# A gated-state attention followed by a SoLU layer on one core: v through a third queue, DMA transposes in the last units, a halved last unit and a new order

## The chip, the cores and the metric

One core of a Trainium2 chip runs the whole program. The metric is the device time of one execution in microseconds (us). The core has five instruction streams: TensorE (PE in the profile, with its weight loads as PEld), VectorE (DVE), ScalarE (ACT), GpSimd (POOL) and SyncE (SP). DMA transfers are issued from the queues of SP, ACT and POOL.

## The reference

```
state = 0                                        # per batch b and head h: 48 x 48
for t in range(768):
    cur   = outer(u * k[t], v[t])
    y[t]  = r[t] @ (state + cur)
    state = w[t][:, None] * state + outer(k[t], v[t])
x  = y, heads side by side                       # 3072 tokens x 384
h  = x @ w_in                                    # 384 -> 1024
s  = h * softmax(h)
ln = (s - mean(s)) / sqrt(var(s) + 1e-6) * g_ln
out = ln @ w_out                                 # 1024 -> 384
```

There are 4 batches, 8 heads, 768 steps and a head size of 48. Everything is given and returned in float32.

## The kernel before

The 768 steps are cut into 6 chunks of 128, which with 4 batches makes 24 units; unit i is batch i mod 4 of chunk i div 4. A unit is 128 tokens of all 8 heads, 384 columns. The recurrence of a chunk becomes matrix products.

- The front of a unit. `LW`, `LK`, `LR`, `LV` load its w, k, r and v (192 KB each, in runs of 192 bytes). `lw` takes the logarithm of w, `cum` sums it over time by two triangular matmuls, `ex` takes the exponential in PSUM, `kp` multiplies it into k and r. `krk` and `krr` transpose the results by head pair on TensorE (four matmuls each), and `kr` copies them out of PSUM. `M` forms the 128 x 128 scores of each head; `m` evicts them, with the mask on DVE, or without it on ACT, and then `sel` masks them on POOL. `p`, `q`, `dg` and `dv` build the bonus of u; `vb` rounds v to bf16. `S`, `et` and `st` advance the state. `Y` multiplies scores and state with v, and `y` evicts it and adds dv (or `Y` adds dv by a matmul with the identity, marked i).
- The back of a unit. `X` transposes y on TensorE and `xT` copies it. `H` is the matmul with w_in into 1024 hidden rows; `e` is their exponential, `he` is h times e, and `hq` its square. `Oa` and `Ob` are the two halves of the last matmul, whose one-column matmuls also sum he, e and hq for the mean, the softmax's sum and the variance. `sq`, `qm` and `lv` turn the sums into a scale, `o` applies it at eviction, and `out` stores 128 rows.
- Once. `LI` and `LO` load w_in and w_out, `wi` rounds w_in, `gw` multiplies w_out by g_ln into w2, `mn` forms the mean over its rows by matmuls, `mc` copies that to SBUF, and `ce` subtracts it from w2 in eight pieces. Every `Oa` needs all of w2. `us` and `uc` spread u over partitions. `hot` issues matmuls on zeros that nothing reads.

The order is written out by hand in the string `ORDER` (L21 to L70) and played by the loop at L522: each word is a stage, its unit, and after the dot the engine or queue (s, a, d, p) or the PSUM slot. The class `InOrder` (L75) chains every instruction behind the one before it on its engine, so nothing on one engine overtakes, DMA issues on that engine's queue included.

Buffers are rings: 7 deep for loaded inputs (`NIO`), 10 for lw and vb, 6 for kp, dv and kr, 4 for the rest (L72). A load of unit i+7 waits until unit i's readers are done. PSUM has single-bank slots s0 to s3 and the two-bank slots b0 and b1. The stages `turned_kr` and `turned_x` (L444 and L447) are defined, but the order before doesn't name them.

Of the kernel before, what the change touches and what calls it, by code (L numbers as in the profile page):

```python
# [8 lines left out]
F32 = mybir.dt.float32  # L9
BF16 = mybir.dt.bfloat16  # L10
# [11 lines left out]
LW0.a LK0.s LU0.a LR0.s LW1.a LW2.s hot4.s3 LG0.s LK1.s lw0 LV0.a cum0.b0 LR1.s us0.s0 ex0 hot2.s3 uc0 lw1 LV1.s  # L22
p0 kp0 LW3.a LK2.a LR2.s krk0.s3 q0 krr0 cum1.b1 kr0.a hot2.s2 LV2.s LK3.a M0.b0 LR3.s p1 gs0.s1 ex1 m0.d
hot3.s3 LI1.s lw2 q1 dg0 cum2.b0 lw3 hot2.s3 kp1 vb0.p LI0.a S0.s2 dv0 vb1.a dg1 hot1.s3 ex2 Y0.is0 et0 LV3.a
cum3.b1 LI2.s p2 kp2 krk1.s3 gc0 LO0.s ex3 st0 LW4.s krk2.s1 q2 krr1 LO1.s krr2 kp3 kr1.a hot3.s2 dv1 LK4.s
kr2.d y0.a p3 M1.b0 LK5.a S1.s2 dg2 krk3.s3 vb2.a m1.d krr3 et1 wi0.a S2.s0 wi1.p M2.b1 st1 X0.s1 kr3.a m2.d
Y1.is2 LR4.s wi2.p et2 y1.a M3.b0 xT0.d LV4.a X1.s3 q3 m3.d H0.b1 dv2 gw1.a dg3 gw2.d e0 Y2.is2 LW5.s xT1.d
gw3.p st2 H1.b0 y2.a he0 lw4 gw0.a X2.s1 LR5.s e1 gw7.d cum4.b1 gw4.d hot2.s3 gw6.d gw5.d ex4 he1 vb3.p mn0.s3
LW6.s LV5.a dv3 xT2.a LK6.s kp4 S3.s0 mc0 Y3.is2 LR6.s lw5 ce6.d krk4.s1 ce3.d hq0.a cum5.b0 ce4.d krr4 ce2.d
H2.b1 ce7.d ex5 LW7.s ce1.d ce5.d ce0.d y3.a LK7.s p4 kp5 et3 Oa0.s3 lw6 e2 LR7.s kr4.d p5 krk5.s2 cum6.b0 st3  # L30
hq1.a Ob0 vb4.p he2 LW8.s q4 krr5 ex6 S4.s1 LK8.s kr5.d sq0 M4.b1 lw7 Oa1.s0 kp6 et4 m4.a LR8.s X3.s2 qm0 st4
vb5.p M5.b0 xT3.a cum7.b1 dg4 sel4 lv0 krk6.s1 LV6.s Ob1 m5.d ex7 LW9.s dv4 lw8 S5.s2 kp7 o0.a krr6 LK9.s p6
cum8.b0 sq1 et5 Y4.ns3 kr6.d ex8 H3.b1 q5 LV7.s y4.d hq2.a kp8 q6 LR9.s krk7.s1 e3 X4.s3 st5 LW10.s vb6.p M6.b0
krr7 xT4.d Oa2.s2 dg5 m6.a LK10.s qm1 kr7.d dv5 krk8.s3 lv1 Ob2 he3 out0 sel6 o1.a lw9 M7.b0 out1 dg6 S6.s1 sq2
m7.a LV8.s hq3.d krr8 cum9.b1 LR10.s Y5.ns0 vb7.p qm2 kr8.d lv2 H4.b0 p7 LW11.s et6 y5.d ex9 st6 p8 lw10 kp9
LV9.s X5.s3 S7.s0 e4 Oa3.s1 q7 o2.d vb8.a he4 out2 cum10.b1 dv6 xT5.a krk9.s2 et7 LK11.s ex10 Y6.ns3 q8 krr9 st7
LV10.s H5.b0 hq4.a kp10 sel7 LR11.s kr9.a y6.d M8.b1 dg7 LW12.s S8.s0 lw11 m8.d Ob3 dv7 et8 e5 LV11.s vb9.p
krk10.s3 st8 X6.s2 LK12.s p9 M9.b1 he5 xT6.a Y7.ns0 sq3 m9.a krr10 LR12.s S9.s2 dg8 cum11.b0 et9 LW13.s y7.d
H6.b1 lw12 dv8 ex11 kr10.d LK13.s p10 qm3 lv3 kp11 Oa4.s0 LR13.s e6 q9 st9 X7.s3 cum12.b0 LW14.s xT7.a Ob4 he6
p11 ex12 LV12.s krk11.s2 sel9 sq4 Y8.ns3 o3.a kp12 H7.b1 hq5.a out3 vb10.p qm4 y8.d q10 LK14.s lv4 dg9 M10.b0 e7  # L40
Oa5.s1 LR14.s m10.d vb11.p q11 o4.a krr11 LW15.s X8.s3 lw13 dg10 Ob5 p12 xT8.a out4 he7 kr11.a S10.s0 dv9 S11.s3
LV13.s dg11 sq5 hq6.a Y9.ns2 vb12.p qm5 cum13.b0 y9.d dv10 LK15.s H8.b1 et10 ex13 st10 LR15.s et11 lw14 kp13
Oa6.s2 LW16.s e8 hq7.d krk12.s0 lw15 M11.b0 p13 st11 LK16.s Ob6 lv5 he8 o5.a q12 krr12 m11.a Y10.ns3 out5 kr12.d
krk13.s1 cum14.b1 LR16.s y10.d sq6 krr13 sel11 ex14 cum15.b0 LW17.s kr13.d Oa7.s0 ex15 qm6 LV14.s kp14 p14
Y11.ns3 lw16 X9.s1 Ob7 kp15 lv6 dv11 LK17.s vb13.a xT9.d p15 o6.a M12.b1 y11.d M13.b0 m12.a X10.s1 out6 m13.d
# [12 lines left out]
e15 X16.s2 o12.d Y17.ns0 xT16.a M18.b0 hq14.a y17.d out12 krk20.s3 Ob13 he15 lw22 X17.s0 m18.a krk21.s2 xT17.d
krr20 cum22.b1 dg19 krr21 sq13 sel18 ex22 qm13 S18.s0 dg20 H16.b0 kr20.d hq15.a q21 kr21.d lv13 kp22 Oa14.s3
dv19 e16 dv20 M19.b1 et18 Y18.ns2 he16 m19.a Ob14 lw23 sel19 y18.d M20.b1 sq14 M21.b0 o13.d Oa15.s2 m21.a st18  # L60
out13 m20.d krk22.s1 X18.s0 cum23.b0 xT18.a krr22 Ob15 ex23 hq16.d vb22.p dg21 kr22.a Y19.ns0 q22 kp23 H17.b1
vb23.a dv21 qm14 sq15 y19.d lv14 Y20.ns1 e17 p23 o14.d H18.b0 dg22 out14 sel21 qm15 y20.d lv15 krk23.s0 he17 e18
Oa16.s3 dv22 krr23 o15.a he18 q23 Ob16 kr23.a out15 X19.s1 M22.b1 xT19.d M23.b0 hq17.d X20.s2 S19.s0 xT20.a
hq18.d Oa17.s1 m22.a dg23 Y21.ns2 et19 m23.a sel22 st19 H19.b1 sq16 sel23 qm16 y21.d lv16 Oa18.s0 e19 dv23
X21.s2 Ob17 he19 H20.b0 sq17 o16.d xT21.d out16 Y22.ns3 qm17 e20 Y23.ns2 y22.d Ob18 y23.d hq19.a he20 H21.b1
lv17 o17.d X22.s3 Oa19.s2 e21 out17 xT22.d hq20.d X23.s1 sq18 H22.b0 he21 xT23.d Ob19 qm18 hq21.d e22 H23.b1
sq19 lv18 qm19 he22 Oa20.s3 e23 o18.d hq22.d Oa21.s1 out18 lv19 he23 Ob20 o19.d Ob21 sq20 hq23.d out19 Oa22.s0
sq21 qm20 qm21 lv20 Oa23.s2 lv21 o20.d o21.d out20 Ob22 out21 Ob23 sq22 qm22 lv22 sq23 qm23 o22.d lv23 out22
o23.a out23
# [27 lines left out]
def kernel(  # L97
# [14 lines left out]
    C = 128  # L112
# [20 lines left out]
    def bank(shape, dtype, slot, name):  # L133
# [6 lines left out]
    v_t = ring("v_in", NIO, [C, H, 64], F32)  # L140
# [8 lines left out]
    dve.memset(warm, 0.0)  # L149
    uti_neg = consts.tile([C, C], BF16)  # L150
    pool.memset(uti_neg, -1.0)
    pool.affine_select(out=uti_neg, in_=uti_neg, compare_op=ALU.is_ge, fill=0.0, base=0,
                       pattern=[[1, C]], channel_multiplier=-1)
    uts = consts.tile([C, C], BF16)
    pool.memset(uts, 1.0)
    pool.affine_select(out=uts, in_=uts, compare_op=ALU.is_gt, fill=0.0, base=0,
                       pattern=[[1, C]], channel_multiplier=-1)
    ident_f = consts.tile([C, C], F32)
    pool.memset(ident_f, 0.0)
    pool.affine_select(out=ident_f, in_=ident_f, compare_op=ALU.not_equal, fill=1.0, base=0,  # L160
                       pattern=[[-1, C]], channel_multiplier=1)
# [394 lines left out]
```

The softmax here doesn't subtract the row's maximum and nothing guards it: scores larger than these inputs give would overflow.

## Time and profile before

| what | value |
|---|---|
| three runs | 152.56, 152.88, 152.94 us; median 152.88 |
| profiled execution | 153.27 us, its span 151.6 us |
| busy PE, DVE, ACT, POOL | 137.2, 127.9, 117.9, 94.9 us |
| first output matmul (w2 ready) | 33.73 us |
| SP issues of v, stores | 20 and 24 |
| bytes moved by DMA | 27.08 MB, 179 GB/s mean |

The span runs from the first to the last recorded instruction; the profiled execution's own time is a little longer. A group line gives busy time and the mean of one instruction, then the idle time of the engine ahead of it with what ended it. The chain of work is followed back from the last instruction, at each step to what released it.

### The profile page before, as it was taken

Reading aid. Unit: us, or ns where it says so; the run is one execution under the profiler, and the core shown is the slowest. Engines: PE = TensorE matmul, PEld = TensorE weight load, DVE = VectorE, ACT = ScalarE, POOL = GpSimd, SP = SyncE. Lnnn points to the kernel's source line nnn. Section 1 sums busy time; section 2 is a strip of 40 time slices with the busy share of each in tenths; the row PEclk is TensorE's granted clock in tenths of the full one; section 3 lists DMA queues with packets and bytes.
Section 4 is the critical chain, followed back from the end, with each engine's and each line's share of the span. In section 5 each row is a group of like instructions: output and inputs, shape, how many; then the busy total and the mean of one; then the engine's idle time right before and its main releaser. Section 6 shows DMA issues by size and latency. Waiting matters only on the chain.

```text
span 151.6 us, 5258 instructions
## 1 busy us (share of the span) xinstructions
PE 137.2 (91%) x2156; PEld 106.6 (70%) x2158; DVE 127.9 (84%) x235; ACT 117.9 (78%) x238; POOL 94.9 (63%) x127
## 2 busy tenths in 40 slices
PE   4799787879999997999988999999999999999980
PEld 1145566467788776888777797878887888889650
DVE  5209797999999996999976999999998998688940
ACT  3465766599999997999798688999898997484442
POOL 7484993531879859993849999299847682500000
PEclk9999999999999999999999999999999999999997
DMA  5999999999983999989699999898950111011142
GB/s 110 259 257 334 405 335 255 178 210 188 224 179 121 229 217 193 215 176 241 142 243 208 230 175 232 162 230 193 248 164 6 52 56 52 4 52 56 52 160 104
DMA packets 104825, 27.08 MB, mean 179 GB/s; under 512 B 100313, under 2 KB 104418, under 8 KB 104802
## 3 DMA queue, kind: packets, MB, share of 16 engines
q1 hardware_dynamic: 94256, 24.26, 69.6%
q10 hardware_dynamic: 10546, 2.49, 7.3%
q8 instruction: 17, 0.28, 0.7%
q14 instruction: 6, 0.05, 0.1%
HBM read 22.03 MB, written 4.72 MB: 176 GB/s over the span
## 4 chain that ended last, share of the span: by engine, by line
PE 54%; DMA 12%; SPq 10%; DVE 8%; ACT 6%; POOL 4%; issue 4%; ACTq 0%; POOLq 0%
PE o_ps L89 22%; PE h_ps L89 13%; SPq L89 10%; DMA w_in<-in_w_dram 6%; PE kr_ps L89 4%; PE y_ps L89 4%; DMA kr_in<-in_r_dram 4%; PE s_ps L89 3%; PE cum_ps L89 3%; PE m_ps L89 3%; DMA v_in<-in_v_dram 3%; PE x_ps L89 2%; DVE he L89 1%; POOL m L89 1%; DVE w L89 1%
## 5 line engine op out<-in xcount | busy, mean ns | idle before, releaser
L89 PE MATMUL o_ps<-w,he 128*128 128x385 bf16 x192 | 45.7, 325 | 0.1
L89 PE MATMUL h_ps<-xT,win_sb 128*128 128x128 bf16 x576 | 35.9, 219 | 0.3 <-DVE xT L89 0.3
L89 PEld LDWEIGHTS <-win_sb 128*128 128x128 bf16 x576 | 33.0, 98 | 0.9 <-issue 0.4
L89 PE MATMUL o_ps<-inv_col,e 128*128 128x1 bf16 x192 | 31.7, 165 | 0.0
L89 DVE TENSOR_TENSOR he<-h_ps,e 128x1024 bf16<-128x1024 f32 x24 | 29.1, 1216 | 2.7 <-ACT e L89 2.5
L89 PE MATMUL o_ps<-one_col,hq 128*128 128x1 bf16 x192 | 31.3, 163 | 0.0
L89 ACT ACTIVATE e<-h_ps 128x1024 bf16<-128x1024 f32 x24 | 24.5, 1020 | 4.7 <-PE h_ps L89 4.6
L89 DVE TENSOR_TENSOR kp<-cum_ps,kr_in 128x768 bf16<-128x768 f32 x24 | 22.7, 948 | 5.9 <-ACT cum_ps L89 5.6
L89 PEld LDWEIGHTS <-hq 128*128 128x128 bf16 x192 | 18.5, 96 | 12.8
L89 POOL TENSOR_TENSOR p<-kr_in 128x384 bf16<-128x384 f32 x24 | 24.4, 1018 | 3.7 <-DMA kr_in<-in_r_dram 3.6
L89 POOL TENSOR_TENSOR dv<-vb,dg 128x384 bf16<-128x384 bf16 x24 | 19.8, 830 | 9.6 <-DVE dg L89 7.4
L89 POOL TENSOR_SCALAR_AFFINE_SELECT m<-m 128x1024 bf16<-128x1024 bf16 x15 | 16.8, 1120 | 13.4 <-ACT sq L89 5.8
L89 POOL TENSOR_TENSOR q<-p,u_bc 128x384 bf16<-128x384 bf16 x24 | 21.8, 911 | 1.9 <-ACT u_bc L89 1.7
L89 PEld LDWEIGHTS <-kp 128*128 128x128 bf16 x272 | 17.4, 98 | 6.0 <-DVE kp L89 2.1
L89 ACT ACTIVATE cum_ps<-cum_ps 128x768 f32<-128x768 f32 x24 | 19.2, 802 | 3.0 <-PE cum_ps L89 2.9
L89 PE MATMUL kr_ps<-ident,kp 128*128 128x128 bf16 x192 | 18.0, 222 | 2.3 <-ACT gr L89 0.8
L89 PEld LDWEIGHTS <-he 128*128 128x128 bf16 x192 | 18.4, 96 | 0.9
L89 PEld LDWEIGHTS <-e 128*128 128x128 bf16 x192 | 18.4, 96 | 0.5 <-issue 0.2
L89 ACT ACTIVATE lw<-w_in 128x384 bf16<-128x384 f32 x24 | 12.4, 523 | 4.1 <-DMA w_in<-in_w_dram 4.1
L89 ACT CAST m<-m_ps 128x1024 bf16<-128x1024 f32 x15 | 15.0, 1013 | 0.7 <-PE m_ps L89 0.6
L89 DVE TENSOR_TENSOR m<-m_ps,keep 128x1024 bf16<-128x1024 f32 x9 | 10.9, 1215 | 4.2 <-PE m_ps L89 4.2
L89 ACT ACTIVATE hq<-he 128x1024 bf16<-128x1024 bf16 x13 | 13.7, 1057 | 0.0
(82 smaller groups left out, 262.5 us busy)
## 6 DMA issues: line engine op xcount, KB each, us to landing
kr_in<-in_r_dram SPq DMA_DIRECT2D x24, 192.0 KB, 4.3
out_dram<-o SPq DMA_DIRECT2D x24, 192.0 KB, 3.2
kr_in<-in_k_dram SPq DMA_DIRECT2D x21, 192.0 KB, 3.5
w_in<-in_w_dram SPq DMA_DIRECT2D x21, 192.0 KB, 4.2
v_in<-in_v_dram SPq DMA_DIRECT2D x20, 192.0 KB, 4.1
wout_f<-in_moe_w_out_dram SPq DMA_DIRECT2D x2, 768.0 KB, 7.7
win_f<-in_moe_w_in_dram SPq DMA_DIRECT2D x2, 512.0 KB, 5.1
v_in<-in_v_dram ACTq DMA_DIRECT2D x4, 192.0 KB, 4.2
```

The lines of the kernel that those rows point to most:

```text
L89: made = make(*args, **kwargs)
```

## The change

- v is loaded 11 times from POOL's queue, 8 times from SP's and 5 times from ACT's, into a tile without padding; it stays float32 and is rounded by `vb` as before. 14 of the stores, two pieces of w_in and one of w_out are issued from POOL as well.
- `centre` reads the column mean from PSUM; its copy to SBUF is gone.
- In units 20 to 23, `KD` and `XD` transpose kp and y by DMA from SP's queue, in place of the matmuls `krk`, `krr`, `X` and the copies `kr`, `xT`.
- Unit 23's back is done in halves: `Ha`, `Hb`, with e, he and hq each in two parts; the sums (`Sa`, `Sb`) go to a PSUM slot of their own ahead of the output matmuls, which are split by columns too (`Mal`, `Mar`, `Mbl`, `Mbr`); ACT and DVE evict one half each, and two stores write them.
- u is rounded to bf16 before it is spread. The constants are set by DVE and only cut to shape by POOL; `keep` is `uts`.
- The order is new throughout. Ahead of the first `Oa` it has `H` up to unit 3 and `cum` up to unit 6 (before: 2 and 5). Dummies: 17 in five groups instead of 19 in eight.

```diff
--- before.py
+++ after.py
...
-LW0.a LK0.s LU0.a LR0.s LW1.a LW2.s hot4.s3 LG0.s LK1.s lw0 LV0.a cum0.b0 LR1.s us0.s0 ex0 hot2.s3 uc0 lw1 LV1.s
-p0 kp0 LW3.a LK2.a LR2.s krk0.s3 q0 krr0 cum1.b1 kr0.a hot2.s2 LV2.s LK3.a M0.b0 LR3.s p1 gs0.s1 ex1 m0.d
-hot3.s3 LI1.s lw2 q1 dg0 cum2.b0 lw3 hot2.s3 kp1 vb0.p LI0.a S0.s2 dv0 vb1.a dg1 hot1.s3 ex2 Y0.is0 et0 LV3.a
-cum3.b1 LI2.s p2 kp2 krk1.s3 gc0 LO0.s ex3 st0 LW4.s krk2.s1 q2 krr1 LO1.s krr2 kp3 kr1.a hot3.s2 dv1 LK4.s
-kr2.d y0.a p3 M1.b0 LK5.a S1.s2 dg2 krk3.s3 vb2.a m1.d krr3 et1 wi0.a S2.s0 wi1.p M2.b1 st1 X0.s1 kr3.a m2.d
-Y1.is2 LR4.s wi2.p et2 y1.a M3.b0 xT0.d LV4.a X1.s3 q3 m3.d H0.b1 dv2 gw1.a dg3 gw2.d e0 Y2.is2 LW5.s xT1.d
-gw3.p st2 H1.b0 y2.a he0 lw4 gw0.a X2.s1 LR5.s e1 gw7.d cum4.b1 gw4.d hot2.s3 gw6.d gw5.d ex4 he1 vb3.p mn0.s3
-LW6.s LV5.a dv3 xT2.a LK6.s kp4 S3.s0 mc0 Y3.is2 LR6.s lw5 ce6.d krk4.s1 ce3.d hq0.a cum5.b0 ce4.d krr4 ce2.d
-H2.b1 ce7.d ex5 LW7.s ce1.d ce5.d ce0.d y3.a LK7.s p4 kp5 et3 Oa0.s3 lw6 e2 LR7.s kr4.d p5 krk5.s2 cum6.b0 st3
-hq1.a Ob0 vb4.p he2 LW8.s q4 krr5 ex6 S4.s1 LK8.s kr5.d sq0 M4.b1 lw7 Oa1.s0 kp6 et4 m4.a LR8.s X3.s2 qm0 st4
-vb5.p M5.b0 xT3.a cum7.b1 dg4 sel4 lv0 krk6.s1 LV6.s Ob1 m5.d ex7 LW9.s dv4 lw8 S5.s2 kp7 o0.a krr6 LK9.s p6
...
-X21.s2 Ob17 he19 H20.b0 sq17 o16.d xT21.d out16 Y22.ns3 qm17 e20 Y23.ns2 y22.d Ob18 y23.d hq19.a he20 H21.b1
-lv17 o17.d X22.s3 Oa19.s2 e21 out17 xT22.d hq20.d X23.s1 sq18 H22.b0 he21 xT23.d Ob19 qm18 hq21.d e22 H23.b1
-sq19 lv18 qm19 he22 Oa20.s3 e23 o18.d hq22.d Oa21.s1 out18 lv19 he23 Ob20 o19.d Ob21 sq20 hq23.d out19 Oa22.s0
-sq21 qm20 qm21 lv20 Oa23.s2 lv21 o20.d o21.d out20 Ob22 out21 Ob23 sq22 qm22 lv22 sq23 qm23 o22.d lv23 out22
+LV0.p pc0 LW0.a LK0.s LW1.a LW2.s hot6.s3 LR0.a LW3.s LU0.a LK1.s lw0 cum0.b0 hot2.s3 LW4.s ex0 lw1 LR1.a
+cum1.b1 hot3.s3 ex1 kp0 p0 LK2.s lw2 ur0 LR2.s krk0.s0 us0.s1 LK3.s cum2.b0 uc0 LV1.a krr0 q0 hot3.s3 LR3.s lw3
+kp1 LV2.a LI0.p ex2 LK4.s p1 dg0 krk1.s2 cum3.b1 vb0.a kr0.d hot3.s3 LR4.s lw4 LI1.p kp2 ex3 dv0 LI2.s LG0.a
+M0.b0 S0.s3 q1 m0.d vb1.a krr1 LW5.s krk2.s1 kr1.a p2 krr2 kp3 et0 LV3.a M1.b0 q2 dg1 kr2.a cum4.b1 krk3.s0 m1.d
+p3 Y0.ns2 krr3 ex4 S1.s1 LO0.s y0.d vb2.p kr3.a LK5.s q3 dg2 S2.s2 st0 wi0.a dv1 kp4 X0.s3 M2.b0 et1 LO1.p xT0.a
+dg3 krk4.s0 wi1.a st1 p4 m2.d Y1.is1 wi2.a LR5.s M3.b1 q4 krr4 gs0.s3 m3.d LW6.s gc0 H0.b0 et2 dv2 vb3.a kr4.d
+y1.a LV4.p lw5 Y2.is3 st2 e0 M4.b1 dg4 dv3 S3.s1 LK6.s y2.a he0 gw3.p Y3.is0 m4.a X1.s2 X2.s3 LR6.s et3 xT1.d
+gw0.a gw1.p cum5.b1 xT2.d H1.b0 st3 y3.a ex5 gw2.d LV5.p gw6.d gw5.a gw4.d gw7.d e1 LW7.s kp5 mn0.s2 he1 LK7.s
+lw6 hq0.a krk5.s3 vb4.p cum6.b1 LV6.p X3.s1 ce1 LR7.s krr5 ex6 H2.b0 ce7 sel4 ce3 kr5.a LW8.s kp6 S4.s0 xT3.a
+dv4 ce0 vb5.a krk6.s3 LK8.s H3.b1 et4 ce5 p5 e2 ce6 LR8.s ce2 p6 LV7.a krr6 ce4 Y4.is1 lw7 he2 e3 q5 LW9.s
+Oa0.s2 vb6.p hq1.a LK9.s he3 M5.b0 q6 Ob0 y4.a LR9.s LV8.p m5.a kr6.d cum7.b1 Oa1.s1 hq2.d ex7 LW10.s sel5 st4
+X4.s3 sq0 M6.b0 lw8 kp7 LK10.s Ob1 xT4.a p7 m6.a qm0 dg5 krk7.s0 LR10.s cum8.b1 hq3.d lv0 krr7 S5.s3 sq1 q7 dg6
...
+Y8.ns1 LW16.s e6 p12 Oa5.s0 y8.d st8 kr12.a LK16.s X7.s1 p13 M11.b0 xT7.d S9.s3 dg11 lw14 LR16.s vb10.p Ob5 he6
+m11.a dv9 S10.s2 et9 LW17.s LV12.p hq6.d cum14.b1 et10 sq5 H7.b0 ex14 qm5 st9 LK17.s q12 st10 lv5 kp14 krk13.s1
...
+lv10 he13 Ob11 dv17 ex20 p20 Y15.ns0 o10.a dg18 H14.b0 hq12.a kp20 q20 lw21 y15.d KD20 krk19.s1 LV20.p sq11 e14
+krr18 qm11 Y16.ns0 kr18.d M17.b1 out10.p krr19 y16.d LK23.s m17.a S15.s2 hq13.d LV21.s Oa12.s0 lv11 kr19.d p21
...
+ex21 out11.p H15.b1 qm12 xT16.a p22 kp21 et16 lv12 S17.s2 e15 hq14.d KD21 Y17.ns1 H16.b0 st16 sel18 vb20.a he15
...
+KD22 lw23 he17 hq16.a Y18.ns3 q23 cum23.b0 Y19.ns2 y18.d ex23 M20.b1 dv20 y19.d Oa16.s3 sq14 m20.a kp23 vb21.p
+X18.s2 vb22.p Ob15 qm14 xT18.d KD23 lv14 dv21 X19.s2 sq15 M21.b0 hq17.d H18.b1 m21.a LV23.s xT19.d sel20 o14.d
...
+Ob17 y20.d qm16 m23.d XD20 lv16 Y21.ns1 sel22 H19.b0 o16.a dg23 sq17 et18 vb23.p y21.d dv23 S19.s3 st18 e19 XD21
+Oa18.s1 et19 he19 Y22.ns2 Ob18 y22.d H20.b1 sq18 qm17 qm18 XD22 st19 lv17 hq19.d Y23.ns2 e20 H21.b0 out16 y23.d
+lv18 XD23 he20 Oa19.s3 e21 hq20.d H22.b1 he21 Ob19 e22 o17.d Ha23.b0 out17 sq19 he22 Oa20.s2 ea23 o18.a qm19
+Hb23 hq22.d hq21.a out18 Ob20 Oa21.s0 sq20 lv19 qm20 hea23 o19.a Oa22.s1 eb23 out19.p Ob21 lv20 heb23 hqa23.a
+Ob22 hqb23.d sq21 qm21 o20.d lv21 Sa23.s3 sq22 out20.p qm22 o21.d Sb23 lv22 Mal23.s2 sq23 o22.a out21.p Mar23.s0
+qm23 Mbl23 lv23 out22 Mbr23 ol23.a or23.d outl23.a outr23
 """
...
-    v_t = ring("v_in", NIO, [C, H, 64], F32)
+    v_t = ring("v_in", NIO, [C, H, D], F32)
...
+    ident_f = consts.tile([KF, KF], F32)
...
+    ones_row = consts.tile([1, C], BF16)
...
+    keep = uts
+
+    def constants(i, x):
+        dve.memset(warm, 0.0)
+        dve.memset(uti_neg, -1.0)
+        dve.memset(uts, 1.0)
+        dve.memset(ident, 0.0)
+        dve.memset(ident_f, 0.0)
+        pool.affine_select(out=uti_neg, in_=uti_neg, compare_op=ALU.is_ge, fill=0.0, base=0,
+                           pattern=[[1, C]], channel_multiplier=-1)
+        pool.affine_select(out=uts, in_=uts, compare_op=ALU.is_gt, fill=0.0, base=0,
+                           pattern=[[1, C]], channel_multiplier=-1)
+        pool.affine_select(out=ident, in_=ident, compare_op=ALU.not_equal, fill=1.0, base=0,
+                           pattern=[[-1, C]], channel_multiplier=1)
+        pool.affine_select(out=ident_f, in_=ident_f, compare_op=ALU.not_equal, fill=1.0, base=0,
+                           pattern=[[-1, KF]], channel_multiplier=1)
+        dve.memset(one_col, 1.0)
+        dve.memset(inv_col, 1.0 / RDF)
+        dve.memset(ones_row, 1.0)
+
+        dve.memset(halves, 0.0)
+        dve.memset(off_blocks, 0.0)
+        for row, own in ((0, 0), (32, 1)):
+            dve.memset(halves[row:row + 1, 64 * own:64 * own + 64], 1.0)
+            dve.memset(off_blocks[row:row + 1, :, 1 - own], -30000.0)
+        for j in range(max(NLW, NKP)):
+            if j < NLW:
+                dve.memset(lw_t[j][:, :, D:], 0.0)
+            if j < NKP:
+                dve.memset(kp_t[j][:, :, :, D:], 0.0)
+        dve.memset(mean_w, -1.0 / DF)
+        dve.memset(w2[:, :, DM:], 1.0 / RDF)
...
-    mean_sb = consts.tile([128, DM], BF16)
...
-    queue = {"s": sp, "a": act}
+    queue = {"s": sp, "a": act, "p": pool}
...
-        queue[x].dma_start(out=v_t[i % NIO][:, :, :D], in_=rows_of(v, i))
+        queue[x].dma_start(out=v_t[i % NIO], in_=rows_of(v, i))
...
+    def round_u(i, x):
+        dve.tensor_copy(out=u_b, in_=u_row)
+
-        pe.matmul(ps["u"], lhsT=ones_row, rhs=u_row, start=True, stop=True)
+        pe.matmul(ps["u"], lhsT=ones_row, rhs=u_b, start=True, stop=True)
...
-    def copy_mean(i, x):
-        act.copy(out=mean_sb, in_=ps["mean"])
-
     def centre(f, x):
-        (dve if x == "d" else pool).tensor_add(out=w2[:, f, :DM], in0=w2[:, f, :DM], in1=mean_sb)
+        dve.tensor_add(out=w2[:, f, :DM], in0=w2[:, f, :DM], in1=ps["mean"])
...
+    def hidden_a(i, x):
+        live[i]["h_ps"] = bank([128, KF, C], F32, x, "h_ps")
+        hidden_part(i, 0, KF // 2)
+
+    def hidden_b(i, x):
+        hidden_part(i, KF // 2, KF)
...
+    def columns_of(i, x, side, part):
+        if part == 0:
+            live[i]["o" + side] = bank([C, DM // 2], F32, x, "o_ps")
+        for f in range(part * KF // 2, (part + 1) * KF // 2):
+            pe.matmul(live[i]["o" + side], lhsT=he_t[i % NWK][:, f, :], rhs=w2[:, f, HALF[side]],
+                      start=(f == 0), stop=(f == KF - 1))
+
+    def sums_of(i, x, part):
+        if part == 0:
+            live[i]["sums"] = bank([C, 3], F32, x, "o_ps")
+        to = live[i]["sums"]
+        for f in range(part * KF // 2, (part + 1) * KF // 2):
+            pe.matmul(to[:, 0:1], lhsT=he_t[i % NWK][:, f, :], rhs=w2[:, f, DM:], start=(f == 0), stop=False,
+                      skip_group_check=True)
+            pe.matmul(to[:, 1:2], lhsT=e_t[i % NWK][:, f, :], rhs=inv_col, start=False, stop=False,
+                      skip_group_check=True)
+            pe.matmul(to[:, 2:3], lhsT=hq_t[i % NWK][:, f, :], rhs=one_col[:, :1], start=False, stop=(f == KF - 1),
+                      skip_group_check=True)
...
+        cols = HALF.get(side, slice(0, DM))
+        queue[x or "s"].dma_start(out=out[b * S + c * C:b * S + (c + 1) * C, cols], in_=o_t[i % NWK][:, cols])
...
```

## The prediction

> **What bounds the kernel now.** I read the page first, then busy time in 4 us stretches, then the chain of work that ended last, then the waits. All instructions are recorded at the helper's line 89, so I go by tiles.
>
> ```profile
> span 151.6 us, 5258 instructions
> PE 137.2 (91%) x2156; PEld 106.6 (70%) x2158; DVE 127.9 (84%) x235; ACT 117.9 (78%) x238; POOL 94.9 (63%) x127
> ```
>
> The stretches, with columns length, then busy us of PE, PEld, DVE, ACT and POOL, granted clock, DMA share and GB/s:
>
> ```profile
> 28.00:32.00 4.00, 2.89 (x33) 1.84 (x32) 3.65 (x8) 2.13 (x5) 2.32 (x3) 1.00 0.98 192
> ...
> 80.00:84.00 4.00, 3.30 (x59) 2.75 (x57) 2.85 (x6) 2.81 (x5) 4.00 (x6) 1.00 0.93 209
> ...
> 104.00:108.00 4.00, 4.00 (x66) 3.40 (x65) 3.96 (x8) 3.67 (x9) 4.00 (x5) 1.00 1.00 219
> ...
> 112.00:116.00 4.00, 4.00 (x77) 3.41 (x75) 3.61 (x7) 3.85 (x9) 3.56 (x4) 1.00 0.09 27
> ```
>
> TensorE is full from 32 to 147 us except for about 2.6 us. DVE is nearly full beside it, and the loads end at 112. Before 32, TensorE has room (2.89 of 4) and the DMA engines don't (0.98). So there are two regimes: supply and weight preparation to 33.7 us, then the length of TensorE's queue. The chain of work shows the border, the price of each stage, and the end (columns: start, us, what):
>
> ```profile
> 30.67 0.49 ACT mean_sb L89
> 31.27 0.45 issue
> 31.72 1.97 DVE w L89 x7
> 33.73 0.99 PE o_ps L89 x12
> ...
> 54.22 0.83 PE o_ps L89 x12
> 55.05 0.24 PE kr_ps L89 x4
> 55.30 0.17 PE x_ps L89 x3
> 55.47 0.33 PE m_ps L89 x8
> ...
> 56.50 0.46 PE s_ps L89 x10
> 56.96 0.33 PE cum_ps L89 x2
> 57.28 1.35 PE h_ps L89 x24
> ...
> 62.03 0.37 PE y_ps L89 x12
> ...
> 140.38 5.98 PE o_ps L89 x84
> 146.38 0.18 ACT sq L89
> ...
> 148.20 0.58 ACT o L89
> ```
>
> The first output matmul (Oa0) starts at 33.73, when w2 is centred. The last unit's sums are read at 147.24 by the timeline, so TensorE ends near 147.1; 4.5 us follow (sums, scale and eviction to 148.78, then the store). From the waits (total us, times, longest):
>
> ```profile
> POOL vb L89 <- DMA v_in<-in_v_dram: 6.1, 4, 2.8
> DVE w L89 <- ACT mean_sb L89: 0.4, 1, 0.4
> ```
>
> v arrives late four times, so supply isn't free even at 80 us, where POOL is full and TensorE is not.
>
> **What the Trainium skill says.** "DMA: Bandwidth & Descriptors", Issuing engines are not separate DMA queues: all queues share 16 engines, and more issuers save only issue time. The trace agrees in part: with SP alone the issues take 0.64 to 1.1 us each back to back at about 200 GB/s, while with two queues the first 12 us hold 257 to 259. "SBUF — State Buffer", Who interferes with whom: descriptors for a GpSimd DMA are written by GpSimd itself and stall while DVE holds the shared port. No run of before issues one.
>
> **The change part by part.** I count TensorE stages at the chain's prices: H 1.34, an output half 0.83, krk or krr 0.225, cum 0.33, S 0.46, M 0.33, Y 0.37, X 0.18.
>
> *Order around Oa0.* Walking the old list from Oa0 to the end gives 107.6 us; the trace took 147.1 - 33.7 = 113.4. The excess of 5.8 (2.6 idle, the rest pipeline bubbles) I keep. The new list puts more before Oa0: one H 1.34, cum 0.33, M 0.33, S 0.46, Y 0.37, X 0.18 and two krk with two krr 0.90, together 3.9 us out of the full regime.
>
> *DMA transposes in units 20 to 23* (KD and XD in the list). Four times krk, krr and X leave TensorE: 4 x (0.45 + 0.18) = 2.5 us, and with them 4 copies of kr and 4 of xT leave ACT and DVE. One more Y adds dv by a matmul, +0.16. The transposes go down SP's queue when loads are over. Neither kind is in the trace. "VectorE: DVE Perf Modes", The three transpose paths, prices one 128x128 block at 1.309 us by DMA. KD has 8 blocks, 1.3 us side by side to 10.5 one after the other; TensorE's work between issue and use is 15.9, 11.5, 7.6 and 4.7 us. XD has 3, 1.3 to 3.9; its cover is 4.2, 3.7, 2.5 and 3.0, less the eviction of y (0.55). The loss is 0 to about 2.5 for XD and 0 to 5.8 for the last KD. A store takes 3.2 us to land, so fixed latency counts: I take 1.0 in all.
>
> *Last unit in halves.* Twelve one-column matmuls at 0.025 each half, 0.5 to 0.6 in all, and 16 half-width ones at 0.083 (half of 0.16 and a little), about 1.4, replace 1.66: +0.24. In return sums, variance and scale (147.24 to 148.2) run beside the main matmuls, and ACT and DVE evict half each. After TensorE's end stand 0.35 for half an eviction (0.58 now) and 2.85 for the store as now (148.78 to 151.6): 3.2 instead of 4.5.
>
> So the list after Oa0 is 107.6 - 3.9 - 2.5 + 0.16 + 0.24 = 101.6, with 5.8 excess 107.4. DVE falls by the same count from 102 to 94, ACT from 95 to 89: neither takes over. Kept at zero: the round of u (DVE idles 3.44 before the first kp, and the matmul falls from fp32's 1.64 to about 0.33) and the constants moved to DVE, in the same idle time. Without that cover they cost some 1.5 us.
>
> *When Oa0 starts.* The second half of w_out now stands behind 21 unit loads instead of 16: 5 x 0.197 MB at 260 to 330 GB/s is 3.0 to 3.8 us. A third queue and an idle SP give part back; I take 2.3, so w_out is ready near 26.5 instead of 24.3 (issued at 16.6 at the latest, 7.7 to landing). DVE's work from there: three gains 1.44, two kp 1.75, one he 1.13, and eight centrings from PSUM. Their nearest row is y<-y_ps,dv, 0.548, start to start 0.47, against 0.30 now: 3.8 us. Sum 8.1, no mean_sb copy and issue (0.94 gone), 0.4 for gaps: Oa0 at 35.0. Bounds are 33 (supply no later, transfers faster) and 39 (all the moved work must wait for unit 6's data).
>
> *v and stores from GpSimd's queue.* SP loses 12 v loads, 15 stores and three weight pieces and gains two other loads, a half store and the transposes; v_in is dense on chip. Supply to vb gets earlier, worth 0 to 2 us (the idle at 76 to 84 is 1.4); I put it against new jitter. The cost lies on POOL: 7 transfers before Oa0 are weights, LV0 and LV4 to LV6, and 18 stand between Oa0 and the last dv. The old emission row doesn't exist. "DMA: Bandwidth & Descriptors", Specifications, gives about 1 us to the first byte for this path and calls it emission; a v load has 1024 runs of 192 B, so I bound it by 0.4 and 3 us and take 1.0. POOL's own work in that stretch is 67.4 (74.2 before); TensorE's is 84.8, with its share of excess 89. The slack is 21.7 us, 1.2 per transfer. At 1.0 POOL is 96% full, and behind a late transfer queue p, q, dv, the masks and vb, for which y, Y and S wait. I charge 1.1 us.
>
> Sum: 35.0 + 107.4 = 142.4 for TensorE's end, + 3.2 = 145.6, + 1.0 transposes + 1.1 POOL = 147.7 for the span. The profiled execution took 153.27 with a span of 151.6, and the median is 152.88, 1.28 above the span: 149.0.
>
> **Rivals.** *GpSimd becomes the bound (slower).* Place: between Oa0 and the last dv. Each us per transfer above 1.2 adds 18 us; without my 1.1 the time is 147.9 + 18e - 21.7, and passes 152.9 at e = 1.48. For it: 1024 short runs per v load, DVE full in 104:108, and stores that wait in POOL's queue for an eviction. Against it: 11 of the 18 are stores with 128 runs. With v loads at 2.6 and stores at 1.1, e is 1.7 and the time about 157.
>
> *The start gives it back.* The front work before Oa0 needs unit 6, and in 28:32 the DMA share is 0.98 at 192 GB/s. If Oa0 slips to 38.5, the time is 152.5, no change. For it: w_out later in every queue. Against it: a third queue.
>
> *Transposes block by block.* Then the cover of the last KD and of XD22 and XD23 fails, 8.3 us in all, and the time is 156. Against it: 7.6 us of cover and more for three of four.
>
> *The changes do more than charged*, supply early and Oa0 at 33: 146.
>
> **How the numbers follow.** Forecast 0.50 (146.8 to 151), start 0.13, GpSimd 0.28, transposes 0.06, more 0.03. Within 0.3%, 152.42 to 153.34, is what a measurement can't tell from none: 0.06, mostly from the start's case. Faster is 0.50 + 0.03 + 0.07 = 0.60, slower 0.28 + 0.06 = 0.34. The range runs from 146 to 157.5: about 0.05 lies below and 0.14 above; the forecast's own range is 146.8 to 151.
>
> **What would show it.** Right: o_ps begins near 35 us, kr_ps and x_ps have 160 and 60 matmuls, PE is full to about 143, and sq of the last unit comes before its last o_ps matmul. Wrong: POOL at 9 in every slice from 35 to 125 us, with PE waiting for dv, m or vb; kr_s or xT released by DMA after 120 us; PE idle before o_ps after 36. A PE gap in the start long enough to halve the clock, now that no dummy stands after unit 3's cum, would also break the sum: matmuls of 384 columns would then take 0.5 us, as they do before 13 us, instead of 0.33.

## The result: slower by 9.5%, and the profile after

The changed kernel takes 167.34 us (median of four runs, 167.09 to 168.38), the kernel before on the same chip 152.91: a ratio of 1.095 (95% interval 1.089 to 1.101). I had predicted 149.0, with 146 to 157.5 as the range. The prediction was wrong by 18 us. Some executions of a kernel take over 1.5% longer than its fastest: the ratios leave these out, the medians don't.

The head of the page of the changed kernel: the span, and the busy time of each engine with its share of the span and its instructions.

```profile
span 165.4 us, 5234 instructions
...
PE 138.8 (84%) x2128; PEld 108.5 (66%) x2128; DVE 139.3 (84%) x238; ACT 119.3 (72%) x245; POOL 113.5 (69%) x139
```

The span grew by 13.8 us. TensorE's busy time grew by 1.6 only, and matmuls that ran at half clock for a while are part of that. DVE gained 11.4 and POOL 18.6. POOL at 69% isn't full, so it isn't simply the new bound. The span falls into three pieces:

| piece | before | predicted | after |
|---|---|---|---|
| first output matmul (Oa0) starts | 33.7 | 35.0 | 46.65 |
| from there to TensorE's end | 113.4 | 107.4 | 115.3 |
| after TensorE's end | 4.5 | 3.2 | 3.5 |
| charged for transposes and POOL | | 2.1 | |
| span | 151.6 | 147.7 | 165.4 |

So 12.9 us were lost before Oa0, 1.9 after it, and 1.0 won at the end. Busy time in 4 us stretches shows the places (columns as in the view of before: length, busy us of PE, PEld, DVE, ACT and POOL, granted clock, DMA share, GB/s):

```profile
24.00:28.00 4.00, 3.05 (x32) 2.13 (x32) 3.13 (x5) 3.47 (x8) 3.44 (x4) 0.50 1.12 300
...
36.00:40.00 4.00, 1.03 (x5) 0.35 (x5) 4.00 (x5) 1.00 (x2) 4.00 (x5) 1.00 0.77 153
...
72.00:76.00 4.00, 0.00 (x0) 0.00 (x0) 4.00 (x1) 0.94 (x2) 3.98 (x6) 0.81 0.90 181
76.00:80.00 4.00, 3.21 (x39) 2.12 (x39) 3.18 (x7) 0.00 (x0) 3.98 (x5) 0.50 1.01 214
```

From 24 to 28 TensorE is busy but at half clock. From 36 to 40 it does next to nothing while DVE and POOL are both full. From 72 to 76 it does nothing at all, and DVE's 4.00 us belong to one instruction; then the clock is at 0.50 again. The chain of work that ended last (here in part) names these instructions (start, us, what):

```profile
13.02 7.65 DMA win_f<-in_moe_w_in_dram
...
20.69 0.38 ACTq L88
...
27.54 2.69 PE h_ps L88 x24
...
31.30 1.23 DVE he L88
...
33.52 5.50 DVE w L88 x4
...
69.15 6.91 issue
76.06 0.69 DVE kr L88
```

The first two lines: ScalarE issues the load LV3 only once a piece of w_in has landed, and its own work stands behind that issue. The third: unit 0's `H` takes 2.69 us where before a `H` took 1.34, the half clock. The fifth: four gains on DVE take 5.50 us; before, the first output matmul began where this line begins. "69.15 6.91 issue" is a time in which DVE waited for nothing that the profile shows. DVE's and POOL's own instructions there, from the timeline of the changed kernel (start, us, engine, operation, tiles):

```profile
68.95 7.18 DVE L88 TENSOR_TENSOR hq<-he 128x1024 bf16<-128x1024 bf16 x1
```

```profile
68.47 0.95 POOL L88 DMA_DIRECT2D v_in<-in_v_dram  x1
69.44 1.11 POOL L88 TENSOR_SCALAR_AFFINE_SELECT m<-m 128x1024 bf16<-128x1024 bf16 x1
70.50 1.95 POOL L88 TENSOR_TENSOR p<-kr_in 128x384 bf16<-128x384 f32 x2
72.40 0.49 POOL L88 CAST vb<-v_in 128x384 bf16<-128x384 f32 x1
...
75.47 1.61 POOL L88 TENSOR_SCALAR_AFFINE_SELECT m<-m 128x1024 bf16<-128x1024 bf16 x1
```

This is unit 5's square (`hq`). All squares on DVE, from the tile's view (shortest/median/longest in ns), first before and then in the changed kernel:

```profile
L89 DVE TENSOR_TENSOR hq<-he x11: 674/681/1419, 46.5 to 143.3; 128x1024 bf16<-128x1024 bf16 x11
```

```profile
L88 DVE TENSOR_TENSOR hq<-he x16: 425/692/7184, 48.9 to 158.9; 128x1024 bf16<-128x1024 bf16 x15, 128x512 bf16<-128x512 bf16 x1
```

The longest took 1.42 us before and takes 7.18 now, beside a median of 0.68 and 0.69. POOL runs nine instructions without a gap over it, and the square ends 0.66 us into the mask at 75.47, which itself takes 1.61 instead of 1.1. This is read as DVE's instruction being held until POOL gave way once. The waits of the changed kernel (total us, times, longest) show who stood behind it, and what came before POOL's close row of work:

```profile
POOL m L88 <- ACT m L88: 9.9, 2, 8.3
...
PE y_ps L88 <- DVE kr L88: 6.2, 1, 6.2
```

TensorE waited 6.2 us for the copy of kr that is next in DVE's order. POOL had waited 8.3 us for a mask's input, while Oa0 was late, and from 49.4 us on worked off what had piled up, nearly without a gap.

### The profile page after: what moved, and what is told of

It reads as the page before. It is cut to its first block, busy times and chain, and to the rows that moved or that the text cites. A ratio compares the mean times of both kernels' runs of the same rounds, so it can differ in the third digit from the quotient of the medians.

```text
span 165.4 us, 5234 instructions
## 1 busy us (share of the span) xinstructions
PE 138.8 (84%) x2128; PEld 108.5 (66%) x2128; DVE 139.3 (84%) x238; ACT 119.3 (72%) x245; POOL 113.5 (69%) x139
## 4 chain that ended last, share of the span: by engine, by line
PE 53%; DVE 18%; issue 8%; SPq 7%; DMA 6%; ACT 5%; ACTq 0%; DVEq 0%
PE o_ps L88 18%; PE h_ps L88 17%; SPq L88 7%; DMA win_f<-in_moe_w_in_dram 5%; PE y_ps L88 4%; PE s_ps L88 3%; DVE w L88 3%; PE m_ps L88 3%; PE kr_ps L88 3%; DVE kp L88 3%; DVE he L88 3%; PE cum_ps L88 2%; DVE st L88 2%; DVE hq L88 2%; DMA kr_in<-in_r_dram 2%
## 5 line engine op out<-in xcount | busy, mean ns | idle before, releaser
L88 PE MATMUL o_ps<-w,he 128*128 128x385 bf16 (+2 forms) x208 | 47.3, 317 | 0.9 <-DVE st L88 0.8
L88 PE MATMUL h_ps<-xT,win_sb 128*128 128x128 bf16 x576 | 38.6, 226 | 0.4 <-DVE m L88 0.4
L88 PEld LDWEIGHTS <-win_sb 128*128 128x128 bf16 x576 | 35.4, 102 | 1.1 <-issue 0.4
L88 DVE TENSOR_TENSOR he<-h_ps,e 128x1024 bf16<-128x1024 f32 (+1 forms) x25 | 29.4, 1175 | 6.1 <-ACT e L88 5.7
L88 ACT ACTIVATE e<-h_ps 128x1024 bf16<-128x1024 f32 (+1 forms) x25 | 24.8, 990 | 7.2 <-PE h_ps L88 6.8
L88 PEld LDWEIGHTS <-hq 128*128 128x128 bf16 x192 | 18.6, 98 | 13.0 <-issue 1.0
L88 DVE TENSOR_TENSOR hq<-he 128x1024 bf16<-128x1024 bf16 (+1 forms) x16 | 20.9, 1308 | 0.1
L88 POOL DMA_DIRECT2D out_dram<-o x14 | 8.2, 584 | 18.5 <-ACT o L88 13.9
L88 PEld LDWEIGHTS <-kp 128*128 128x128 bf16 x240 | 15.7, 99 | 7.4 <-DVE kp L88 4.8
L88 PE MATMUL kr_ps<-ident,kp 128*128 128x128 bf16 x160 | 15.7, 226 | 2.8 <-DVE kp L88 2.8
L88 PEld LDWEIGHTS <-kr 64*128 64x128 bf16 (+1 forms) x272 | 10.7, 97 | 10.1 <-issue 7.3
```

What stands on the lines that cost most here:

```text
L88: made = make(*args, **kwargs)
```

## The experiments

Theory A: DVE is held off by POOL, whose work has no gaps now that it issues 18 transfers as well (`hq` and the gains are what is held); a second, independent part is the start, where ScalarE and DVE have too much ahead of Oa0. Rival B: POOL itself is too slow with its transfers, as my second case had it. Rival C: the new order is the loss, wherever the transfers are issued. Ratios are to the kernel before on the same chip, spans from the profiled execution.

**The queue alone.** Ten v loads and the fourteen stores go back to SP, all else stays.

```diff
-... LV4.p ... LV5.p ... out0.p ... out21.p
+... LV4.s ... LV5.s ... out0.s ... out21.s
```

> The changed kernel with 10 of its 11 v loads and all 14 stores of GpSimd's queue put on SP's, at the same places in the order. Port theory (a DVE instruction with two SBUF inputs is held off while GpSimd runs without a gap): GpSimd gets gaps, the square of unit 8 falls from 7.18 us to under 1.5, and the time from 167.3 to about 158. Rival, the order itself (the new places of the work make the gaps vanish, whoever issues): the square stays over 4 us and the time over 164.

Measured: 155.79 us, ratio 1.008 (1.006 to 1.011), span 154.3. TensorE ends at 150.9, 106.0 us after Oa0 at 44.9. DVE's squares in this kernel, from the tile's view (shortest/median/longest in ns):

```profile
L89 DVE TENSOR_TENSOR hq<-he x16: 424/692/1433, 47.1 to 147.8; 128x1024 bf16<-128x1024 bf16 x15, 128x512 bf16<-128x512 bf16 x1
```

No square is long (the expectation calls the one of 7.18 us unit 8's; it is unit 5's), and 8.7 of the 9.5% are gone. So transfers on POOL's queue cost nearly all of it, and rival C falls in that form. What is left is the start: Oa0 only came from 46.65 to 44.9, and DVE's four gains still take 3.49 us.

**Which DVE work is held.** Three runs move work away from DVE in the changed kernel. The first was badly aimed: it moves the squares of units 8 and 18, but the long ones are those of 5 and 14. It serves as a control.

```diff
 first:  -hq8.d hq18.d          +hq8.a hq18.a
 second: -gw2.d gw6.d gw4.d gw7.d   +gw2.a gw6.a gw4.a gw7.a
 third:  -hq5.d hq14.d          +hq5.a hq14.a
```

> The changed kernel with the squares of units 8 and 18 on ACT instead of DVE; every transfer stays where it is. Port theory: 6.5 + 1.7 us of DVE time and the half clock after the long one go, ACT pays twice 1.06; about 158 to 160. Rival, GpSimd is simply full and late (my slower case): its work is untouched, so 166 or more.

Measured: 170.28 us, ratio 1.099 (1.093 to 1.106). Unit 5's square takes 8.14 us. Two squares fewer on DVE bring nothing, where 158 to 160 us had been expected: DVE's load by itself isn't it.

> The changed kernel with DVE's four gains on w_out (5.58 us in a row beside a GpSimd without gaps) on ACT. Port theory: ACT does them in about 2.6 us, the first output matmul comes 2 to 3 us earlier than 46.6, the time is about 164.5. Rival: w2 is late for what comes before the gains, and ACT's backlog takes the gain; no change.

Measured: 165.56 us, ratio 1.071 (1.067 to 1.075); Oa0 at 43.9, unit 5's square still 7.18. ScalarE does the gains that DVE couldn't get done, which brings Oa0 2.8 us forward; the rest of the loss stays.

> The changed kernel with the squares of units 5 and 14 on ACT: these, not 8 and 18, are the two that took 7.18 and 2.43 us on DVE. Port theory: neither is held off any more, ACT pays 1.06 each, and TensorE keeps its clock at 72 to 84 us; 7 to 9 us less, a ratio to the kernel before of 1.04 to 1.05 instead of 1.095. Rival, the hold-up passes on to the next square (unit 6 or 15), since GpSimd is as full as it was: a ratio over 1.08 and another square over 3 us.

Measured: 162.73 us, ratio 1.055 (1.046 to 1.065). The longest square left is 2.23 us, though the gains took 7.59 in this run and Oa0 came at 49.6. So a large part of the loss is the wait of these two instructions, and it doesn't come back at the same length in another square.

**The start.** Two runs relieve ScalarE in the changed kernel: LV3 from SP, and in the second also two roundings of w_in on POOL.

```diff
 first:  -LV3.a   +LV3.s
 second: -LV3.a wi1.a wi2.a   +LV3.s wi1.p wi2.p
```

> The changed kernel with the load of v for unit 3 on SP's queue instead of ACT's. Theory: ACT stands 3.3 us behind its own transfer at 17.8 to 21.1, TensorE runs dry 2.85 us and drops to half clock from 22 to 30; without it the clock stays full and the first output matmul comes 4 to 6 us earlier, the time is about 162. Rival: ACT waits for w_in's bytes in any case, and the time stays within 1 us of 167.3.

Measured: 162.75 us in one run and 166.11 to 166.14 in the three others, of which one was profiled: span 164.4, Oa0 at 44.7. One run is too few for a ratio.

> The changed kernel with the start relieved: v of unit 3 loaded from SP, and two of the three roundings of w_in on GpSimd, as in the kernel before, instead of ACT. Theory: ACT's row of transfer, copies and roundings at 17.8 to 27 makes the first hidden matmul start at 27.5 instead of 21.8; it comes near 24, at full clock, and the first output matmul 3 to 5 us before 46.6: a ratio of 1.06 to 1.075. Rival, the bytes of w_out are the limit of the start: no change, 1.09 or more.

Measured: 163.89, 165.52, 167.63 and 167.99 us, so no ratio can be told here either; in the profile Oa0 is at 44.2. Both relieved kernels win some 2 us before Oa0, not the 3 to 6 expected: the gains on DVE begin 1.7 and 0.5 us earlier and take 5.37 and 3.69 us instead of 5.58, still far over the 1.44 of the sum. Both also keep a square of 8.1 us. ScalarE's stand behind its own load is gone, but the half clock isn't, though the expectation took it to follow from TensorE's dry 2.85 us. Of the second run:

```profile
24.00:28.00 4.00, 3.23 (x32) 2.32 (x33) 3.40 (x4) 1.45 (x5) 4.00 (x6) 0.50 1.13 344
```

No gap of TensorE between 14.1 and 24 us is longer than 0.66 us in this profile. With the queue's hold-up gone, the same relief was tried again, with the gains on ScalarE, and then with eight dummies ahead of unit 0's `Y` on top.

```diff
 both:   -LV3.a wi1.a wi2.a gw2.d gw6.d gw4.d gw7.d ... LV4.p ... out0.p ...
         +LV3.s wi1.p wi2.p gw2.a gw6.a gw4.a gw7.a ... LV4.s ... out0.s ...
 second: -Y0.ns2   +hot8.s2 Y0.ns2
```

> The changed kernel with ten v loads and all fourteen stores on SP's queue (as in the run that did this alone), and with the start relieved: LV3 on SP's queue instead of ScalarE's, wi1 and wi2 on GpSimd, the gains gw2, gw4, gw6 and gw7 on ScalarE instead of DVE. If what is left of the loss (ratio 1.008) is DVE's and ScalarE's queues ahead of the first output matmul, that matmul comes about 4 us earlier, near 41 us, and the ratio is about 0.98. If it is the amount of work that the new list puts ahead of it, at half clock, it stays at 44 or later and the ratio at 1.00 to 1.01.

> The same, with eight dummies ahead of unit 0's Y. If the half clock between 22 and 30 us follows from TensorE's dry stretch near 20 us, the dummies keep the clock at 1.00 there, and the first output matmul comes 2 to 3 us before that of the kernel without them. If the clock falls anyway, or the supply of data sets the pace, there is no gain, or up to 1.5 us of loss for the dummies' own time.

Measured: 154.59 us, ratio 0.999 (0.991 to 1.006), Oa0 at 42.5; with dummies 154.14, ratio 0.997 (0.989 to 1.005), Oa0 at 41.9. The half clock from 24 to 32 is gone in both; the first has a shorter one before it (0.88 from 16 to 20 and 0.70 from 20 to 24), the second has 1.00 throughout. The relief is worth 2.4 us before Oa0 and the dummies 0.6 more, within what these runs can tell. Neither is told apart from the kernel before, where a ratio of 0.98 was hoped for: in the second Oa0 is 8.2 us later than before, and TensorE needs 106.7 us after it instead of 113.4. The new order's start and its shorter rest cancel.

**The old order.** Two runs use the changed kernel's code with the order of before (`pc0` first, `ur0` before `us0`, no `mc0`). The first adds the halved last unit and the DMA transposes; the second instead puts the ten loads and fourteen stores on POOL's queue.

```diff
first:
-... krk20.s3 krr20 kr20.d ... X20.s2 xT20.a ... Oa23.s2 ... o23.a out23
+... KD20 ... XD20 ... Sa23.s2 ... Mal23.s3 ... Mbr23 ol23.a or23.d outl23.a outr23
second:
-... LV4.a LV5.a LV6.s ... out0 ... out21
+... LV4.p LV5.p LV6.p ... out0.p ... out21.p
```

> The order of before with the rest of the change that doesn't need GpSimd's queue: constants, u and mean as changed, DMA transposes for units 20 to 23, and the last unit's sums and columns split. Sum of the prediction's terms: 2.5 us of TensorE's queue for the transposes and 1.3 - 0.24 for the end, about 3.5 us less, a ratio of 0.975 to 0.98. Rival, transposes come late in the tail: the end gives 1 us, the ratio is 0.99 to 1.0.

Measured: 155.13 us, ratio 1.008 (1.005 to 1.011). The end is 3.1 us (3.1 to 3.8 in all halved kernels), but Oa0 slipped to 36.8: ScalarE's gain waited 4.2 us for w_out and the clock was halved until 34.

> The order of before with the same 10 v loads and 14 stores on GpSimd's queue as in the change (no transposes, whole last unit). Port theory needs only that GpSimd loses its gaps: with 24 transfers at 0.58 to 0.95 us more, some two-input squares are held off, and the ratio is 1.01 to 1.04. Rival, the hold-up comes from the new order alone: no square over 1.5 us and a ratio of 0.99 to 1.005.

Measured: 157.72 us, ratio 1.022 (1.014 to 1.031), Oa0 at 33.2. From the timeline of this kernel, DVE near 88 us:

```profile
88.36 4.40 DVE L90 TENSOR_TENSOR hq<-he 128x1024 bf16<-128x1024 bf16 x1
```

POOL ran from 80.27 to 92.2 without a gap, and its last transfer before this square ended at 80.25, 8.1 us ahead of it. The queue brings the hold-up without the new order. And this run's Oa0 at 33.2, with no dry spell, points to a use of the queue that helps: only the three early loads.

**Without a gap, or with transfers?** The first run takes the transfers off POOL as above and puts useless work of nearly the same length in each one's place. The second takes just LV11 and LV12, which POOL issues during unit 5's square, off its queue.

```diff
 first:  -LV4.p ... out0.p    +LV4.s jv4 ... out0.s jo0
 +    def stand_in_v(i, x):
 +        one = u_bc.rearrange("t h d -> t (h d)")
 +        pool.tensor_mul(out=junk[0], in0=one, in1=one)
 +    def stand_in_o(i, x):
 +        pool.tensor_copy(out=junk[1], in_=o_t[i % NWK])
 second: -LV11.p ... LV12.p   +LV11.s ... LV12.s
```

> The changed kernel with its ten v loads and fourteen stores on SP's queue, and in the place that each had on GpSimd a piece of useless work of about the same length (a 128x384 product, 0.9 us, for a v load; a 128x384 copy of o, 0.5 us, for a store). If DVE is held off because GpSimd has no gap between instructions, whatever they are, a square of 3 us or more comes back near 69 or 124 us and the ratio is 1.03 or more. If it is something that a transfer's issue does, all squares stay under 1.5 us and the ratio stays near the 1.01 of the run without the stand-ins.

Measured: 156.30 us, ratio 1.016 (1.008 to 1.024). DVE at unit 5's square, and POOL at the same time, from the timeline of this kernel:

```profile
68.36 1.37 DVE L90 TENSOR_TENSOR hq<-he 128x1024 bf16<-128x1024 bf16 x1
```

```profile
68.09 1.09 POOL L90 TENSOR_SCALAR_AFFINE_SELECT m<-m 128x1024 bf16<-128x1024 bf16 x1
69.15 2.40 POOL L90 TENSOR_TENSOR p<-kr_in 128x384 bf16<-128x384 f32 x2
```

POOL is without a gap from 61.5 to 85 us here, and still the square got in at POOL's first change of instruction: the two products took 2.40 us instead of 1.95. So theory A, as I put it, falls. A gapless POOL alone doesn't hold DVE off for more than one instruction.

> The changed kernel with only LV11 and LV12 on SP's queue, the two v loads that GpSimd issues inside unit 5's square of 7.18 us. If that square waits for the end of one gapless train of GpSimd's instructions, taking two links (1.9 us) out makes a gap and the square falls under 2 us; the time falls by 5 to 7 us, ratio about 1.05. If many small delays add up, it falls by 2 us at most.

Measured: 168.82 us, ratio 1.091 (1.082 to 1.100). Unit 5's square takes 7.98 us. Nine of POOL's compute instructions follow each other over it with no transfer among them; it ends 0.60 us into the tenth, the next load. So transfers inside the train aren't needed either.

**Loads or stores.** In the changed kernel, the first run takes the fourteen stores off POOL, the second the ten v loads.

```diff
 first:  -out0.p ... out21.p   +out0.s ... out21.s
 second: -LV4.p ... LV22.p     +LV4.s ... LV22.s
```

> The changed kernel with its fourteen stores on SP's queue; the ten v loads stay on GpSimd's. If the v loads (1024 runs of 192 bytes each) are what makes GpSimd win the shared port again and again, a square of 5 to 8 us stays near unit 5, and the ratio is 1.06 or more. If the stores do it, or if GpSimd waiting for a store's eviction is what puts its work so close together, all squares stay under 1.6 us and the ratio is 1.01 to 1.03.

> The changed kernel with its ten v loads on SP's queue; the fourteen stores (128 runs of 1536 bytes each) stay on GpSimd's. By the first reading the squares stay under 1.6 us and the ratio is 1.01 to 1.03; by the second a square of several us stays and the ratio is 1.05 or more. If long squares appear in both, any transfer on GpSimd's queue is enough.

Measured: 162.69 us, ratio 1.064 (1.054 to 1.075), longest squares 2.21 and 2.67 us; and 165.33, ratio 1.078 (1.073 to 1.083), longest square 7.97. From the timeline of the second, DVE and then the first and last of POOL's instructions during the square:

```profile
66.69 7.97 DVE L89 TENSOR_TENSOR hq<-he 128x1024 bf16<-128x1024 bf16 x1
```

```profile
66.21 1.09 POOL L89 TENSOR_SCALAR_AFFINE_SELECT m<-m 128x1024 bf16<-128x1024 bf16 x1
...
74.07 1.35 POOL L89 TENSOR_TENSOR q<-p,u_bc 128x384 bf16<-128x384 bf16 x1
```

Either kind is enough, and the stores, which keep POOL for 0.58 us each, do at least as much as the v loads with 0.95. The first reading, that the v loads make the long square, fits the ratio only: with them alone no square reaches 3 us. The last line again is POOL's instruction that gave way, 1.35 us for 0.91. What is shown, by one profile of each kernel: in all ten kernels that issue stores, v loads or both from POOL's queue throughout (the changed one is one of them) some square takes 2.2 to 8.1 us, and in the ten others, before included, none takes more than 1.45. What is open: why POOL then wins the change of instruction up to eight times running. The stand-ins show that it isn't the length of its work, and the square in the old order that no transfer need be near; the trace has no field that shows more. ScalarE's queue in place of SP's wasn't tried.

**What can be kept.** Four runs in the old order with the halved last unit and only LV4, LV5 and LV6 on POOL's queue: without and with the transposes, and both again with LV14 moved three loads earlier in SP's queue, because its late landing left TensorE dry near 80 us.

```diff
-LV4.a ... LV5.a ... LV6.s      +LV4.p ... LV5.p ... LV6.p
 third and fourth:
-LK16.s ... LR16.s ... LW17.s ... LV14.s
+LV14.s LK16.s ... LR16.s ... LW17.s
```

> The changed kernel's code with the order of before, the last unit in halves, TensorE's own transposes in every unit, and only LV4, LV5 and LV6 on GpSimd's queue (with LV0's place as before). If the start of the run with the whole queue in the old order (first output matmul at 33.2) came from these three loads being off SP's and ScalarE's queues, the first output matmul comes at 33 to 34, there is no long square on DVE later, and the time is 1 us under before: ratio 0.990 to 0.996. If those three are enough to hold DVE off, the gains are long and the ratio is over 1.00.

> The same with the DMA transposes of units 20 to 23. By the prediction's sum they take 2.5 us from TensorE and cost at most 1.0 in lateness: 1.5 to 2.5 us less than the kernel without them, ratio 0.975 to 0.985. If late blocks give it back, as the rival has it, the two are within 0.5 us or this one is slower.

Measured: 153.42 us, ratio 0.989 (0.978 to 0.999), without transposes; 152.65, ratio 0.987 (0.979 to 0.995), with them. Oa0 is at 33.2 and 33.4. The second of these differs from the run with transposes above (1.008, Oa0 at 36.8) in nothing but the queue of the three loads: they are worth about 2%. The transposes showed no gain that can be told, since TensorE's idle time between 76 and 84 was 0.7 us in the first profile and 3.1 in the second.

> The kernel with before's order, the halved last unit and three v loads on GpSimd's queue, with LV14 moved three loads earlier in SP's queue (ahead of LK16 instead of behind LW17). If the idle time of TensorE near 80 us is that load coming last, 1.5 to 2.5 us go and the ratio is about 0.975. If SP's queue only shifts the lateness to the loads that it is moved past, the ratio stays at 0.99.

> The same with the DMA transposes of units 20 to 23. With supply no longer late at 80 us, the 2.5 us of the transposes should show if TensorE's list bounds the end: 1.5 to 2.5 us less than the kernel without them. If the two are within 0.5 us, the transposes give TensorE nothing that it can use, or load the DMA engines with as much as they save.

Measured: ratio 0.985 (0.980 to 0.989), span 148.9, without transposes; 0.979 (0.974 to 0.985), span 149.5, with them. The two are not told apart. TensorE's idle time near 80 is down to 0 and 0.1 us. Both are faster than the kernel before, by 1.1 to 2.7% over both intervals, and so than the changed one. The profile of the last shows where most of the 2.5 us of the transposes goes. Its waits of TensorE between 100 and 130 us, and the stretch around one of them:

```profile
PE m_ps L89 <- DMA kr<-kp: 1.5, 1, 1.5
```

```profile
112.00:116.00 4.00, 3.03 (x56) 2.17 (x53) 2.66 (x5) 2.98 (x8) 3.51 (x5) 1.00 1.02 229
```

The scores wait 1.5 us for a KD, and from 108 to 120 TensorE idles 1.9 us, where it idles not at all in the kernel without transposes. The DMA engines are still full there with the last loads.

## Why the prediction was wrong, point by point

**When Oa0 starts (35.0, was 46.65): failed.** I let DVE's work begin when w_out is ready, at 26.5. But in DVE's order the gains stand behind `he` of unit 0, which waits for `H`, for three roundings of w_in on ScalarE, and for ScalarE's own issue of LV3. They began at 33.44: 6.9 us. The supply term was off too, without deciding this: POOL issued the second half of w_out behind its own work at 23.0, not by 16.6, and 5.7 us to landing make it about 29. Then DVE took 12.2 us instead of 8.1, since the four gains took 5.58 where I had counted 1.44 for three: 4.1 us. About half of that isn't the queue, since they took 3.49 with the transfers on SP's. TensorE's order took 1.0 after that instead of 0.4. The rest of the term was right: eight centrings from PSUM at 0.541 us each, 3.9 against my 3.8. My rival for the start had the direction but was far too small, and my last sentence named the half clock without putting a price on it.

**TensorE's list after Oa0 (107.4, was 115.3): right count, wrong cover.** With the transfers off POOL's queue it took 106.0. The 3.9 us moved ahead and the 2.5 of the transposes are really gone from it. The other 9.3 us, and 1.75 of what was lost before Oa0, are the step on POOL's queue.

**v and stores from GpSimd's queue (1.1, was some 11 us): failed in its mechanism.** I priced the time that a transfer keeps POOL, at 1.0 us from a page's time to the first byte. It takes 0.58 for a store and 0.95 for a v load, less than I charged. "GpSimd becomes the bound" would have needed 1.48 and was wrong as well, though its time, 157, erred in the right direction. The step that failed is that the sum kept DVE's instructions at their old length beside a POOL with 18 transfers more. The cost is there: squares of 0.68 us took up to 8.1. I had read the very rule. "SBUF — State Buffer", Who interferes with whom, says that a DVE instruction with two inputs in SBUF contends with a GpSimd instruction that reads SBUF, and that whoever issues first blocks the other. I used it only in the direction of DVE delaying descriptors, which no run here shows. `hq` has two inputs in SBUF, and the trace of before already had one at 1.42 instead of 0.68. I could have bounded the cost from that row, but the page's rule gives one instruction of POOL as the longest wait, where these runs show up to nine. Here the measurement decides.

**Half clock: named, not priced.** "TensorE: Matmul & The Clock Gate", HAM oscillation, warns of idle gaps over about 3.4 us. The wait at 72 was longer, 6.2 us, and was followed by four us at 0.50 and four at 0.84: 3.21 x 0.50 and 4.00 x 0.16, 2.2 us of work lost on top of the wait. In the start the longest gap was 2.85 us, and some 6 us at half clock followed; but they came as well in the run whose gaps there were 0.66 us at most. So I can't say what halves the clock in the start; eight dummies, together with the other relief, kept it at 1.00.

**After TensorE's end (3.2, was 3.5): right.** The halved last unit is worth 1.0 us of the 4.5 here, and 0.7 to 1.4 in the other kernels that have it.

**Transposes (2.5 won, 1.0 lost): right in the changed kernel, not in the old order.** There the median from issue to landing was 3.1 us for KD and 2.3 for XD, and no wait of the trace is for them, so "Transposes block by block" was wrong: eight blocks in 3.1 us, against an estimate of 10.5 from "VectorE: DVE Perf Modes", The three transpose paths. In the old order KD met the last loads, and TensorE idled 1.9 us, most of the 2.5 won.

## What to carry to other kernels

Before moving DMA issues to GpSimd's queue, list the DVE instructions that already take longer beside GpSimd's work (here products of two SBUF tiles and scalings of float32 to bf16), and price the move by their waits, not by GpSimd's busy time alone; three early loads from that queue were a gain here. The start of a term is the last of everything ahead of it in that engine's written order, not the arrival of its data. A shorter list for the bounding engine is worth nothing if as much time is added ahead of the point where its full regime begins.

## What the runs showed of the hardware that I had not expected

- A DVE product of two bf16 tiles in SBUF (0.68 us) waited through up to nine consecutive GpSimd instructions, 7.2 to 8.1 us in seven and 2.2 to 4.4 in three kernels that use GpSimd's queue throughout, and never more than to the first change of instruction (1.45 us) in those that don't.
- Gains on DVE (128x384, float32 to bf16, 0.41 us each in the fastest kernel) took up to 3.0 us each in the changed kernel, while GpSimd had no gap.
- A DMA issue keeps GpSimd for 0.58 us with 128 runs of 1536 bytes and 0.95 us with 1024 runs of 192 bytes.
- ScalarE stood 3.3 us behind its own issue of one 192 KB load while 512 KB pieces of w_in were under way, and didn't where that load was on SP's queue.
- TensorE's clock was at 0.50 from 24 to 30 us in a run whose gaps in the ten us before were 0.66 us at most.
